# New tables for the split of softmax tiles between ScalarE and VectorE, and for the places of FFN and output tiles

## The chip, the cores and the metric

The kernel runs on one core of a Trainium2 chip. The metric is the device time of one execution in microseconds (us). Before the change three runs took 757.08, 756.82 and 756.5 us, with a median of 756.82 us.

A core has a matrix engine (PE, with its weight loads shown as PEld), VectorE (DVE), ScalarE (ACT), GpSimd (POOL) and SyncE (SP), which here issues DMAs. Each engine works through its own list of instructions in order, and waits on semaphores for the others.

## What is computed

One transformer block in parallel form, with S = 2048 rows, D = 512, 32 heads of 16 that share one K and one V, and a GELU layer of width F = 1792:

```python
xn = layernorm(x)
q = (xn @ wq)            # 32 heads of 16
k, v = xn @ wk, xn @ wv  # one head of 16, shared
p = softmax(q @ k.T * 16 ** -0.5)
attention = (p @ v) @ wo
ffn = gelu(xn @ w1 + b1) @ w2 + b2
out = x + attention + ffn
```

Inputs and output are bf16. The exponentials of the softmax are the largest part: 32 x 2048 x 2048 of them.

## The kernel before

**Tiles and units.** Scores are made transposed, a tile having 128 keys and 512 queries of one head. There are four blocks of 512 queries, eight groups of four heads in each, and 64 tiles to a group (16 blocks of keys by four heads): 2048 tiles. Three tiles make a unit, and there are 683 units. `scores` (L933) puts a unit into three of six PSUM banks with three matmuls (L947) on different rows of PE; units alternate between the two halves of the six banks, so the scores of unit u + 2 cannot start until those of unit u have been read.

**Two ways to an exponential.** A tile is read by ACT or by DVE. ACT applies Exp to all its tiles of a unit in one instruction (L970), one to three tiles wide, and writes bf16 to `E`. DVE takes a different way: L1001 adds a constant to the scores, clamps them and writes int16 to `Dt`, whose bits read as bf16 are a power of two with a straight line in place of the curve. To mend the curve, the weighted sum of five such tiles with different offsets is used. DVE makes the offset copies with integer additions on whole batches (L1047): first one copy of the batch, then, from two copies, two more at once. The last step (L1044) changes one tile at a time in its place, and can go to POOL or to DVE. So a batch of n tiles costs one L1047 of width n, one of width 2n and n instructions of L1044.

**The matmuls with V.** L1014 multiplies a tile by V into one of four column groups of PSUM bank 6. An ACT tile takes one such matmul, a DVE tile five, with V scaled by five different constants.

**The table.** `DTAB` (L60) is a string with one character for each unit, which says which of its tiles go to DVE (`DMASK`, L57): `.` none, `0`, `o` the first, `2`, `t` the last, `a`, `A` the first two, `b`, `B` the last two, `x`, `X` all three. The characters of `CLOSE` (L59: `o`, `t`, `A`, `B`, `X`) end the batch. A batch also ends at six tiles (`KB`) and at the last DVE tile of a group of 64.

**Side work.** Between the units, the kernel does the rest of the block with PSUM bank 7: the projections of q (`q_pack`, L1117), the FFN tiles (`h_mm`, L1146: 16 matmuls and one evacuation by DVE, L1150; 14 of them for each block of 512 queries, 56 in all), and the output tiles (`out_tile`, L1191, and `y_tile`, L1201: the second FFN matmul, the projection of the attention output, the bias and the addition of x; 16 in all). `HP` (L73) and `YP` (L74) hold the unit from which each FFN tile and each output tile may start; an operation placed at u depends on unit u's exponential. x for an output tile is loaded by SP six units ahead. GELU runs on ACT for two blocks at a time, behind units 182 and 512 (`GU`, L75); the FFN tiles of blocks 0 and 1 have to be evacuated by the first, and those of 2 and 3 by the second. No exp of a later unit runs before it.

**The order.** All this is written down as operations with what they read and write. `schedule` (L224) then plays the five engines forward in time with a table of durations and a due time for each operation, and fixes the order of every engine's list; that includes whether an L1044 goes to POOL or to DVE: it may go to POOL beside a DVE instruction that reads PSUM, and DVE takes it where nothing is due earlier. Where PE would be idle for long it adds matmuls with zeros (L1318). The order is fixed when the program is built, and on the chip it cannot adapt.

Of the kernel before, what the change touches and what calls it, by code (L numbers as in the profile page):

```python
# [56 lines left out]
DMASK = {".": (), "0": (0,), "2": (2,), "a": (0, 1), "b": (1, 2), "x": (0, 1, 2),  # L57
         "o": (0,), "t": (2,), "A": (0, 1), "B": (1, 2), "X": (0, 1, 2)}
CLOSE = "otABX"  # L59
DTAB = "20t0220t2..o.02ttt.o.22.to0.2.ot00t2.tt20t.too..222ot2.t.t0.tt2tt0o2.tto.o.ott..oto2ot22.000t0..oot.ot00o.tooot0t.t.200o.0.2o2t..ooo2o20o.ot.o0o..02o..20t2..20tto0o.222o..2220oto02tA2bAoooo02t2o.t22ootoo202oo.22t.tto0t02.o20.o2.to00to..0tto0o22oo22.2tt2o.to0.0toot.tt02.t.2ooo.t202o.t00o0.t2.o22t.0oto00t020o2..o000o0oo.2...02ot00.oo...b...o.2.tt.ooo.0.22at.0t0o.t200.22toob...0t.to..ttto0t..2ootoot02.o0.o..oo2t0to0.ooo2..t02o2.20toot0.o.t220.A.o.0o0.ot.t2.2to0ott20o.2.2222o0.22.0o2ot2...ot.tt..20t02200o00..o.2X2XoBtooo2tt20tt..0o.o0t0t.o.2t2ooto2t.to22tt0t.t.o0o00o.o0.ottt2o200to.2o00.o220.o.2ttt2o2o0.0t02.t0o2.t.2ot.0to0t.2ot02o202o.2.o0ooot2t202o.0oo..o2oo.02tt.22o2.t.2o.o.."  # L60
YF = 664
Y_ALLOW = 8.0
H_ALLOW = 5.0
# [6 lines left out]
EXP_LAT = 0.16  # L70
Q3 = (7, 4, 2)
QK = ((48,88.7,157.4),(45,107.7,130.4),(62,118.7,159.4))
HP = ((15,19,24,26,34,41,45,46,50,52,52,63,81,89),(70.14,86,105.29,106.71,130.86,132.29,141,142.57,157.43,161.86,164.71,167.43,169.14,177.57),(290.86,291,302,305.29,307.71,324.14,341.43,344.57,345.86,358.57,372.71,377.29,378.43,389.14),(428.86,430.14,444,444.43,457.57,458.71,461.14,461.86,466.29,472.57,473.43,479.71,481.29,491))  # L73
YP = ((196,221,243,281),(347,373,383,413),(520,528,530,589),(601,635,641,654))  # L74
GU = ((182, (0, 1)), (512, (2, 3)))  # L75
FG = 7
UB2 = 2
# [449 lines left out]
def bass_parallel_sum__grouped_kv_mqa__dense_activation_gelu__prompt_kernel(  # L527
# [33 lines left out]
    with ExitStack() as es:  # L561
# [584 lines left out]
        def h_mm(tb, ft, ev=EV_ALLOW):  # L1146
            for d in range(DT):
                mm4(pM, w1_sb[:, d, ft * P:(ft + 1) * P], xnT[:, d, tb * TBW:(tb + 1) * TBW], d == 0, d == DT - 1,
                   r=["w1"] + tr(4 * tb, 4 * tb + 4), w=[B(7)], allow=H_ALLOW if tb < NTB - 1 else 1.5)
            dve(lambda e: e.tensor_scalar(ubs[tb % 2][:, ft, :], pM, b1T[:, ft:ft + 1], None, ALU.add),  # L1150
                r=["b1T"], w=M4 + [ukey(tb, ft)], n=TBW + 57, allow=ev)
# [20 lines left out]
        def wo_mm(tb, i, ps, start=False, bk=7, al=1.5):  # L1172
            for n, p in enumerate(ps):
                pp = tb * NGR // 2 + p
                hs = [h for h in range(2) if 2 * pp + h < NTB * NGR - 1]
                assert all(2 * pp + h in onorm for h in hs) and 2 * (pp + NPR) + 1 not in onorm
                mm4(bank(bk), oTp[:, pp % NPR, i * P:(i + 1) * P], wop[:, p, :], start and n == 0, False,
                   r=[("oTp", pp % NPR), "wop"], w=[B(bk)], allow=al)
# [4 lines left out]
        def x_load(tb, i):  # L1183
            ti = tb * 4 + i
            dma("sp", x_sb[:, 14 + i % 2, :], x_view[:, ti, :], f"d_xr{i % 2}", w=[("x", 14 + i % 2)], lat=2.5)
# [5 lines left out]
        def out_tile(tb, i):  # L1191
            y_mm(tb, i, al=Y_ALLOW)
            wo_mm(tb, i, range(NGR // 2), al=Y_ALLOW)
            b2_mm(al=Y_ALLOW)
            xr, key = x_sb[:, 14 + i % 2, :], ("x", 14 + i % 2)
            dve(lambda e: e.tensor_tensor(xr, pM, xr, ALU.add), w=[key] + M4, allow=EV_ALLOW)
            store(tb, i, xr, key)
# [3 lines left out]
        def y_tile(tb, i):  # L1201
            y_mm(tb, i, al=YT_ALLOW[i])
            wo_mm(tb, i, range(FIN_G), al=YT_ALLOW[i])
            b2_mm(stop=i < 3, al=YT_ALLOW[i])
            xr, key = x_sb[:, 14 + i % 2, :], ("x", 14 + i % 2)
            if i < 3:
                dve(lambda e: e.tensor_tensor(xpy[:, i, :], pM, xr, ALU.add), r=[key],
                    w=M4 + [("u", 0, 2 * i), ("u", 0, 2 * i + 1)], allow=EV_ALLOW)
            else:
                mm4(pM, ident, xr, False, False, r=["ident", key], w=[B(7)], allow=YT_ALLOW[i])  # L1210
# [9 lines left out]
        def at(u, fn, cost=0.0):  # L1220
            side.append((u, len(side), fn, cost))

        def q_at(tb, p, u, ps=(), hqs=(), gls=(0, 1)):
            at(u, lambda: q_pack(tb, p, gls), 0.93)
            if ps:
                at(u + 1.5, lambda: q_m(ps, hqs), 0.6)
# [6 lines left out]
        for tb in range(NTB):  # L1233
            u0 = tb * UPT
            if tb > 0:
                for i in range(4):
                    at(YP[tb - 1][i] - 6, lambda tb=tb, i=i: x_load(tb - 1, i))
                    at(YP[tb - 1][i], lambda tb=tb, i=i: out_tile(tb - 1, i), 0.6)
                q_at(tb, 3, u0 + Q3[tb - 1], (2, 3), (4, 5, 6, 7))
            for ft in range(FT):  # L1240
                at(HP[tb][ft], lambda tb=tb, ft=ft: h_mm(tb, ft), 0.66)
            if tb + 1 < NTB:
                for k in range(3):
                    q_at(tb + 1, k, u0 + QK[tb][k], (0, 1) if k == 1 else (), (0, 1, 2, 3))
            else:
                for i in range(4):
                    at(YP[tb][i] - 6, lambda tb=tb, i=i: x_load(tb, i))
                    at(YP[tb][i], lambda tb=tb, i=i: y_tile(tb, i), 0.6)
                at(YF, lambda tb=tb: wo_mm(tb, 3, range(FIN_G, NGR // 2), al=WF_ALLOW))
        side.sort(key=lambda s: (s[0], s[1]))  # L1250

        for u, c in enumerate(DTAB):
            for i in DMASK[c]:
# [5 lines left out]
        for t in range(NTILE):  # L1259
            if is_d[t]:  # L1260
                first, n = (t, 1) if n == 0 else (first, n + 1)
                if n == KB or last_d[t // TPG] == t or (DTAB[t // 3] in CLOSE and not any(is_d[t + 1:t // 3 * 3 + 3])):
                    bsize[first], n = n, 0
# [93 lines left out]
```

## Time and profile before

| what | us |
|---|---|
| three runs | 757.08, 756.82, 756.5 |
| median of the runs | 756.82 |
| span of the profiled execution, first to last instruction | 3410.1 |
| PE busy in it | 3402.4 |
| DVE busy in it | 795.2 |
| ACT busy in it | 808.8 |
| POOL busy in it | 306.0 |

No time of the profiled execution beside its span is given. The page shows a granted TensorE clock of 1.000 for it. Busy time of an engine is the time covered by at least one of its records; a group of instructions is given with its line, engine, operation, tile written and tile read, shapes, count, busy time in us, mean duration in ns, and the idle time of its engine ahead of it with what ended that.

### The profile page before, as it was taken

What the parts mean: (1) busy time and instruction counts of PE and PEld (TensorE: products, weight loads), DVE (VectorE), ACT (ScalarE), POOL (GpSimd) and SP (SyncE); (2) the same over time, 40 slices, a digit from 0 to 9 for tenths busy, and PEclk for the clock granted to TensorE, in tenths of its full rate; (3) what the DMA queues carried; (4) which work ended last, traced back from release to release, by engine and by line L of the source; (5) the groups of instructions that cost most, each with busy time, mean ns of one, the idle gap of its engine ahead of it and who ended that gap; (6) DMA issues with size and microseconds to landing.
All of it is one profiled execution on the core that took longest, in us unless ns stands there. A gap on an engine that the chain in (4) does not pass through costs nothing.

```text
span 3410.1 us, 21709 instructions
## 1 busy us (share of the span) xinstructions
PE 3402.4 (100%) x8948; PEld 426.5 (13%) x8950; DVE 795.2 (23%) x1511; ACT 808.8 (24%) x747; POOL 306.0 (9%) x444
## 2 busy tenths in 40 slices
PE   9999999999999999999999999999999999999999
PEld 4101111111120011001111111101111101111112
DVE  2222222222222222222222222222222222222221
ACT  2222222222222222222222222222221222222221
POOL 1101011110001111110000000000010011110000
DMA  2000000000000000000000000000000000000000
GB/s 82 2 4 7 3 2 4 3 5 4 5 4 3 7 5 8 2 5 5 5 8 5 5 5 1 8 2 7 4 1 12 5 2 7 5 7 5 7 3 7
DMA packets 32075, 23.31 MB, mean 7 GB/s; under 512 B 16369, under 2 KB 27498, under 8 KB 31978
## 3 DMA queue, kind: packets, MB, share of 16 engines
q1 hardware_dynamic: 30922, 21.90, 2.4%
q8 instruction: 71, 1.16, 0.1%
q14 instruction: 26, 0.21, 0.0%
q10 hardware_dynamic: 1056, 0.03, 0.0%
HBM read 13.08 MB, written 2.35 MB: 5 GB/s over the span
## 4 chain that ended last, share of the span: by engine, by line
PE 99%; issue 1%; ACT 0%; DVE 0%; POOL 0%; POOLq 0%
PE pAll L1014 50%; PE pAll L947 27%; PE pAll L661 19%; PE pAll L655 2%; PE pAll L1318 1%; PE pAll L799 1%; PE pAll L1316 0%; PE pAll L1110 0%; ACT xnT L804 0%; DVE x_sb L1150 0%; PE pAll L887 0%; ACT ub L1311 0%; ACT oTp L833 0%; DVE kmr L889 0%; POOL ident L686 0%
## 5 line engine op out<-in xcount | busy, mean ns | idle before, releaser
L1014 PE MATMUL pAll<-Dt,V 128*32 128x512 bf16 x2720 | 1911.2, 1580 | 0.0
L970 ACT ACTIVATE E<-pAll 128x1024 bf16<-128x1024 f32 (+1 forms) x681 | 757.1, 1112 | 2428.9 <-PE pAll L947 2416.5
L1014 PE MATMUL pAll<-E,V 128*32 128x512 bf16 x1504 | 1209.8, 1522 | 0.0
L947 PE MATMUL pAll<-QT,KT 32*128 32x512 bf16 x2048 | 999.4, 1427 | 0.0
L1001 DVE TENSOR_SCALAR Dt<-pAll 128x512 int16<-128x512 f32 (+1 forms) x532 | 374.1, 703 | 2163.6 <-PE pAll L947 2152.3
L1044 POOL TENSOR_SCALAR Dt<-Dt 128x512 int16<-128x512 int16 x389 | 289.5, 744 | 2995.4 <-DVE Dt L1047 1157.5
L661 PE MATMUL pAll<-xnT,w_sb 128*32 128x512 bf16 x896 | 547.7, 1592 | 0.9 <-DVE x_sb L1150 0.9
L661 PE MATMUL pAll<-w_sb,x_sb 128*32 128x512 bf16 x448 | 321.1, 1597 | 0.0
L661 PE MATMUL pAll<-w_sb,ub 128*32 128x512 bf16 x448 | 310.8, 1591 | 0.0
L947 PEld LDWEIGHTS pAll<-QT,KT 32*128 32x128 bf16 x2048 | 98.3, 122 | 1660.5 <-issue 1468.4
L1047 DVE TENSOR_SCALAR Dt<-Dt 128x1024 int16<-128x1024 int16 (+6 forms) x582 | 289.5, 525 | 2.1 <-PE pAll L1014 1.6
L1014 PEld LDWEIGHTS pAll<-Dt,V 128*32 128x32 bf16 x2720 | 203.0, 160 | 666.8 <-issue 625.4
L661 PE MATMUL pAll<-wop,oTp 128*32 128x512 bf16 x256 | 238.8, 1589 | 0.0
L1014 PEld LDWEIGHTS pAll<-E,V 128*32 128x32 bf16 x1504 | 112.4, 143 | 259.8 <-issue 252.4
L661 PE MATMUL pAll<-xnT,wq_sb 128*32 128x512 bf16 x256 | 115.3, 1594 | 0.0
L661 PEld LDWEIGHTS pAll<-xnT,w_sb 128*32 128x32 bf16 x896 | 68.2, 190 | 144.7 <-issue 134.3
L661 PE MATMUL pAll<-b2row,ones 128*32 128x512 bf16 x64 | 83.3, 1618 | 0.0
L1318 PE MATMUL pAll<-xnT,zeros 128*32 128x512 bf16 x84 | 49.2, 1559 | 0.0
L1150 DVE TENSOR_SCALAR ub<-pAll,b1T 128x512 bf16<-128x512 f32 x28 | 21.0, 750 | 107.4 <-PE pAll L661 56.9
L661 PEld LDWEIGHTS pAll<-w_sb,x_sb 128*32 128x32 bf16 x448 | 38.9, 182 | 46.5 <-issue 46.5
L1150 DVE TENSOR_SCALAR x_sb<-pAll,b1T 128x512 bf16<-128x512 f32 x28 | 21.0, 749 | 86.3 <-PE pAll L661 57.0
L1044 DVE TENSOR_SCALAR Dt<-Dt 128x512 int16<-128x512 int16 x155 | 39.4, 283 | 5.9 <-PE pAll L1014 5.9
(120 smaller groups left out, 423.6 us busy)
## 6 DMA issues: line engine op xcount, KB each, us to landing
OfP<-Of SPq DMA_DIRECT2D x124, 32.0 KB, 1.9
rbP<-rden_rows SPq DMA_DIRECT2D x124, 32.0 KB, 1.8
w_sb<-in_B_w_dram SPq DMA_DIRECT2D x2, 1792.0 KB, 12.0
x_sb<-in_A_x_dram SPq DMA_DIRECT2D x8, 256.0 KB, 4.3
x_sb<-in_A_x_dram SPq DMA_DIRECT2D x16, 128.0 KB, 2.1
QT<-qp SPq DMA_DIRECT2D x124, 16.0 KB, 1.8
out_dram<-x_sb SPq DMA_DIRECT2D x12, 128.0 KB, 1.7
wq_sb<-in_A_wq_dram SPq DMA_DIRECT2D x1, 512.0 KB, 6.2
```

Source lines behind the costliest of these rows:

```text
L655: return add("pe", lambda e: e.matmul(o, l, rh, start=start, stop=stop, **kw), r, w, occ=occ, lat=0.23, allow=allow, **ak)
L661: add("pe", lambda e, c=c, j=j: e.matmul(o[c, :], l[:, c], rh, start=start, stop=stop, tile_position=(0, 32 * j)), r, [(k, j) for k in w] ...
L799: add("pe", lambda e, ti=ti, d=d, o=o: e.transpose(pT[:, o:o + P], xn[:, ti % 8, d * P:(d + 1) * P], ident[:]), r=[("u", 0, ti % 8), "iden ...
L947: ins = e.matmul(o, l, rh, start=True, stop=True, tile_position=(q0, 0))
L970: o = act(lambda e: e.activation(E[:, s0:s0 + na, :], bank(b0, na).rearrange("p (a n) -> p a n", a=na), ACT.Exp, scale=LN2 / 128.0), w=[B( ...
L1001: op = dve(lambda e: e.tensor_scalar(Dt[:, s:s + n, :], bank(bk, n).rearrange("p (a n) -> p a n", a=n), float(127 * 128) + SPL_D, SPL_MIN, ...
L1014: add("pe", lambda e, a, b: e.matmul(pO[32 * j:32 * j + 32, :], V1[:, v, kt, :], rhs, start=a, stop=b, tile_position=(0, 32 * j)), r=r + [ ...
L1044: add("pool", lambda e, d=d, k=k: e.tensor_scalar(d, d, 1.0, float(k), ALU.mult, ALU.add), [], [(("D", base[o > 0] + q), o)], occ=PL_OCC, ...
L1047: dve(lambda e, d=view(o, nb), q=view(i, nb), k=k: e.tensor_scalar(d, q, float(k), None, ALU.add), r=keys(i), w=keys(o), n=nb * n * TBW, m ...
L1150: dve(lambda e: e.tensor_scalar(ubs[tb % 2][:, ft, :], pM, b1T[:, ft:ft + 1], None, ALU.add), r=["b1T"], w=M4 + [ukey(tb, ft)], n=TBW + 57 ...
L1318: pr.filler = lambda e, j, o: e.matmul((pO if o else pM)[32 * j:32 * j + 32, :], zeros[:, 0:32], xnT[:, 0, 0:TBW], start=not o, stop=not o ...
```

## The change

Three tables of constants are replaced. `DTAB` has a new string of the same length, 683 characters; `HP` and `YP` have new starting units, 14 for each block of queries in `HP` and four for each block in `YP`. No function is changed. The starting units of the projections of q (`QK`, `Q3`), the units of GELU and all costs and due times of the planner stay.

```diff
-DTAB = "20t0220t2..o.02ttt.o.22.to0.2.ot00t2.tt20t.too..222ot2.t.t0.tt2tt0o2.tto.o.ott..oto2ot22.000t0..oot.ot00o.tooot0t.t.200o.0.2o2t..ooo2o20o.ot.o0o..02o..20t2..20tto0o.222o..2220oto02tA2bAoooo02t2o.t22ootoo202oo.22t.tto0t02.o20.o2.to00to..0tto0o22oo22.2tt2o.to0.0toot.tt02.t.2ooo.t202o.t00o0.t2.o22t.0oto00t020o2..o000o0oo.2...02ot00.oo...b...o.2.tt.ooo.0.22at.0t0o.t200.22toob...0t.to..ttto0t..2ootoot02.o0.o..oo2t0to0.ooo2..t02o2.20toot0.o.t220.A.o.0o0.ot.t2.2to0ott20o.2.2222o0.22.0o2ot2...ot.tt..20t02200o00..o.2X2XoBtooo2tt20tt..0o.o0t0t.o.2t2ooto2t.to22tt0t.t.o0o00o.o0.ottt2o200to.2o00.o220.o.2ttt2o2o0.0t02.t0o2.t.2ot.0to0t.2ot02o202o.2.o0ooot2t202o.0oo..o2oo.02tt.22o2.t.2o.o.."
+DTAB = "t2t22t00202t..22tt..022.to00.t22t00200..o.t..20222o.o2.tot22.2t.t2222tt22..2o222t2..o202o02tt2.o.2.t0.t202.2.20t0toto.2..0ot.t2..ot0o2t02t.2222o.0t...o0ot2020o2.2t0.02.t00.02.20o002..xxXaoto.02oot.0to2tt.0too0.ot0tot.o0o020t0o0.tt20.t22.o0tto..2t2to220oo.22t0.2ooo.o2t2o.0ot0o.t02t022.to0..oot.2t2t.o0002ot.0.2tto.0tt2.02t0.202t.2t.oo.ot0.00t.t0o0.0o0o..o0o22o2.00.t0tot2.0o2.2o.t2o2o.tt22o.0t.0oo.2ot2t2.o0.t0t20to2.2t0t.tt2t.002tt.oo.o0oooo0.2o0o0.t00t2ot2.0t0tt0.oA.o..020tt2t02..t0000...2o..02ot0020o.t2t...00XbXttto200t.tt0o22tt..0t0t222.o2o2.t2t20.t0t0.t0t00t2o.0tt2tot.t000202t2t.o.0to20.0.2o22t0o.2t00o0t0..t02o0.0o.o0ooto.t2t0to.2oo0o222o0022o00.2t.2..t0t2.2t.tttt2.2.to.o.."
-HP = ((15,19,24,26,34,41,45,46,50,52,52,63,81,89),(70.14,86,105.29,106.71,130.86,132.29,141,142.57,157.43,161.86,164.71,167.43,169.14,177.57),(290.86,291,302,305.29,307.71,324.14,341.43,344.57,345.86,358.57,372.71,377.29,378.43,389.14),(428.86,430.14,444,444.43,457.57,458.71,461.14,461.86,466.29,472.57,473.43,479.71,481.29,491))
-YP = ((196,221,243,281),(347,373,383,413),(520,528,530,589),(601,635,641,654))
+HP = ((14.33,26.29,49.54,147.27,14,38.77,51.6,14,34.61,92.18,56.17,130.88,103.7,49),(108.69,82.59,66.39,104.08,133,93.7,109.35,162.93,173.36,139,171.29,159.02,133,137.17),(308.62,328.89,290.1,325,306.98,336.81,316.24,310.73,293.91,381.46,369.7,349,374.48,453.6),(475,473.57,427,468.62,459.3,464.72,451,455.66,491.16,486.09,482.33,480.6,464.72,461.37))
+YP = ((195.26,184.23,228.93,254.61),(353.39,411.43,387.54,421),(516,530.79,566.23,553.42),(600.53,607,655.32,660.47))
```

## The prediction, as it was written before the change was run

> **What bounds the kernel now.** I read the page's head and its chain first, then the groups of ScalarE and VectorE with their shapes kept apart, then the order of time in two short stretches.
>
> ```profile
> span 3410.1 us, 21709 instructions
> ...
> PE 3402.4 (100%) x8948; PEld 426.5 (13%) x8950; DVE 795.2 (23%) x1511; ACT 808.8 (24%) x747; POOL 306.0 (9%) x444
> ...
> PE 99%; issue 1%; ACT 0%; DVE 0%; POOL 0%; POOLq 0%
> ```
>
> The span is 3410.1 us and the three timed runs have a median of 756.82 us. PE's records fill the span, and 3402 us of them cannot lie in a run of 757 us. So PE ran at least some 3402.4 / 756.8 = 4.5 times slower in the profiled execution than in the runs, and the chain, 99% PE, is the chain of that execution alone. No other time of that execution is given; I use its durations on ACT, DVE and POOL as prices, work out differences between the two kernels, and add them to the median of the runs. The waits of this trace are no guide to the runs.
>
> What fills 757 us is seen by adding the records of each engine.
>
> ```profile
> L970 ACT ACTIVATE E<-pAll 128x1024 bf16<-128x1024 f32 x523 | 535.1, 1023 | 1890.8 <-PE pAll L947 1878.5 <-PE pAll L1014 9.3 <-PE pAll L655 2.8
> L970 ACT ACTIVATE E<-pAll 128x1536 bf16<-128x1536 f32 x150 | 217.5, 1450 | 520.3 <-PE pAll L947 520.3
> ...
> L970 ACT ACTIVATE E<-pAll 128x512 bf16<-128x512 f32 x8 | 4.7, 596 | 17.8 <-PE pAll L947 17.8
> ```
>
> ```profile
> 33.76 0.81 ACT L781 ACTIVATE ub<-x_sb,nmr,rstd 128x512 bf16<-128x512 bf16 x1
> 34.47 0.19 ACT L769 ACTIVATE rstd<-lnv 128x2 f32<-128x2 f32 x1
> ```
>
> Back to back, a record on ACT begins before the one ahead of it ends: 33.76 + 0.81 = 34.57, but the next starts at 34.47, 0.10 us earlier. The 681 exps, back to back, then hold ACT for 523 x 0.923 + 150 x 1.350 + 8 x 0.496 = 689 us. All else on ACT (GELU, its table loads, the LayerNorm at the start) is 808.8 - 757.3 = 52 us: some 741 us in all. Of 756.8 us only 16 are left, for the start before x has landed, the end and every wait. **ACT is the first bound.**
>
> The same for DVE, whose rows are these:
>
> ```profile
> L1001 DVE TENSOR_SCALAR Dt<-pAll 128x512 int16<-128x512 f32 x522 | 360.8, 691 | 2108.1 <-PE pAll L947 2104.3 <-PE pAll L655 3.1 <-remote 0.6
> L1047 DVE TENSOR_SCALAR Dt<-Dt 128x1024 int16<-128x1024 int16 x222 | 89.9, 418 | 0.1
> L1047 DVE TENSOR_SCALAR Dt<-Dt 128x2048 int16<-128x2048 int16 x90 | 61.4, 683 | 0.1
> L1047 DVE TENSOR_SCALAR Dt<-Dt 128x3072 int16<-128x3072 int16 x46 | 43.7, 951 | 0.1
> L1047 DVE TENSOR_SCALAR Dt<-Dt 128x512 int16<-128x512 int16 x150 | 41.3, 283 | 0.1
> L1044 DVE TENSOR_SCALAR Dt<-Dt 128x512 int16<-128x512 int16 x155 | 39.4, 283 | 5.9 <-PE pAll L1014 5.9
> L1047 DVE TENSOR_SCALAR Dt<-Dt 128x1536 int16<-128x1536 int16 x41 | 22.5, 550 | 0.1
> L1047 DVE TENSOR_SCALAR Dt<-Dt 128x4096 int16<-128x4096 int16 x18 | 21.8, 1218 | 1.6 <-PE pAll L1014 1.6
> ...
> L1150 DVE TENSOR_SCALAR ub<-pAll,b1T 128x512 bf16<-128x512 f32 x28 | 21.0, 750 | 107.4 <-PE pAll L661 56.9 <-PE pAll L1014 50.4
> ...
> L1001 DVE TENSOR_SCALAR Dt<-pAll 128x1024 int16<-128x1024 f32 x8 | 9.8, 1224 | 43.3 <-PE pAll L947 43.3
> L1047 DVE TENSOR_SCALAR Dt<-Dt 128x6144 int16<-128x6144 int16 x5 | 8.8, 1751 | 0.0
> ...
> L1047 DVE TENSOR_SCALAR Dt<-Dt 128x5120 int16<-128x5120 int16 x5 | 7.4, 1474 | 0.0
> ...
> L1047 DVE TENSOR_SCALAR Dt<-Dt 128x2560 int16<-128x2560 int16 x5 | 4.1, 819 | 0.0
> ...
> L1001 DVE TENSOR_SCALAR Dt<-pAll 128x1536 int16<-128x1536 f32 x2 | 3.5, 1757 | 12.3 <-PE pAll L1014 7.6 <-PE pAll L947 4.7
> ```
>
> ```profile
> L1044 POOL TENSOR_SCALAR Dt<-Dt 128x512 int16<-128x512 int16 x389 | 289.5, 744 | 2995.4 <-DVE Dt L1047 1157.5 <-PE pAll L1014 733.5 <-DVE Dt L1001 646.5
> ```
>
> ```profile
> 1001.54 0.69 DVE L1001 TENSOR_SCALAR Dt<-pAll 128x512 int16<-128x512 f32 x1 [3.12 <-PE pAll L947]
> 1002.15 0.42 DVE L1047 TENSOR_SCALAR Dt<-Dt 128x1024 int16<-128x1024 int16 x1
> ...
> 1022.03 0.68 DVE L1047 TENSOR_SCALAR Dt<-Dt 128x2048 int16<-128x2048 int16 x1
> ...
> 1022.20 0.99 POOL L1044 TENSOR_SCALAR Dt<-Dt 128x512 int16<-128x512 int16 x1 [6.43 <-DVE Dt L1001]
> ...
> 1027.29 0.62 POOL L1044 TENSOR_SCALAR Dt<-Dt 128x512 int16<-128x512 int16 x1 [4.10 <-DVE Dt L1001]
> ```
>
> On DVE the overlap is 1001.54 + 0.69 - 1002.15 = 0.08 us; over the 269 pairs of L1001 and L1047 its median is 0.083. Less this for each instruction, reading scores (L1001) costs 522 x 0.608 + 8 x 1.141 + 2 x 1.674 = 330 us, the additions of L1047 257 us and the 155 of L1044 on DVE 31 us; and all of DVE is at least the page's 795.2 - 1511 x 0.083 = 670 us (the page counts overlapped time once, so this takes off too much). So **DVE is close behind ACT**. But 31 us of it, L1044, can go to POOL, where 389 of 544 already run: DVE has work that it can shed.
>
> **The change part by part.**
>
> *Tiles.* I counted both tables by the rules of the code: characters to tiles, batches closed at six tiles, at a closing letter or at the end of a group. For the table of before this gives exactly the counts of the rows above. For the new one: VectorE tiles 544 to 555; exps of two tiles 523 to 535, of three 150 to 140, of one 8 to 3 (units without an exp: 2 to 5).
> ACT: 12 x 0.923 - 10 x 1.350 - 5 x 0.496 = **-4.9 us**.
> DVE, L1001: singles 522 to 534, pairs 8 to 3, triples 2 to 5: 12 x 0.608 - 5 x 1.141 + 3 x 1.674 = +6.6 us.
> DVE, L1047: 291 batches become 274. By width in units of 512: one 150 to 116, two 222 to 204, three 41 to 38, four 90 to 105, five 5 to 9, six 46 to 44, eight 18 to 17, ten 5 to 9, twelve 5 to 6. At the rows less 0.083: -6.8 - 6.0 - 1.4 + 9.0 + 2.9 - 1.7 - 1.1 + 5.6 + 1.7 = +2.1 us. DVE in all: **+8.6 us** that only DVE can do.
> L1044: 11 more tiles; 0.20 us each on DVE (2.2 us), or 0.62 us each on POOL, whose 306 us leave it room. Which of the 555 go where isn't written in the diff (the planner decides); from none to all 155 on DVE I take a shift to POOL that covers most of the 8.6 us: 8.6 / 0.20 = 43 tiles.
> PE: 11 tiles more by five matmuls in place of one, 44 more in four column groups, 11 waves.
>
> ```profile
> 1005.51 2.55 PE pAll L1014 x2
> ```
>
> Two waves of L1014 in the chain took 2.55 us, 1.28 each; by the factor 4.5 at most 0.28 in a run. 11 waves: between 0 and +3.1 us. I take 0, as PE's share of the runs isn't known and ACT and DVE fill theirs.
> For that the Trainium skill ("TensorE: Matmul & The Clock Gate", section "Wait — 56ns, not 53.3ns?") has 215.7 ns between 512-column matmuls at full clock, by which the 11 waves would be an estimated 2.4 us; the trace, at 1.28 us a wave, doesn't agree and no row here shows such a rate.
>
> *Positions.* All 72 pieces of side work stay, with the same matmuls, evacuations and DMAs; only the unit from which the planner may start them moves. Where they fall decides whether DVE's sum fits under ACT's in each stretch. I put prices from the rows on each unit (exps and GELU for ACT; L1001, L1047 and evacuations at their positions, 0.667 us for an FFN tile and some 0.6 for each other, for DVE), added both over successive stretches, and summed the greater. Over stretches of 5, 10, 20 units this gives 799.0, 763.4, 738.2 before and 792.5, 754.2, 730.0 after: -6.5, -9.2 and -8.2. With a quarter of L1044 on DVE (155 of 544 are 28%) the differences are -5.7, -9.5 and -6.3. These totals are not times, since buffers of two units of scores, and some 19 tiles behind them, smooth more or less than that; but the sign holds for each stretch. Cost of the moves themselves: 0, hidden under ACT as long as each FFN tile is evacuated ahead of the GELU at units 182 and 512. The last start ahead of 182 goes from 177.57 to 173.36, ahead of 512 from 491 to 491.16. If that cover went, each late evacuation would hold ACT 0.67 us (0.750 less the overlap).
>
> *Sum.* ACT gives -4.9 and the stretches at least -5.7; I take -5.3, between them, as ACT is the bound that no buffer relieves: 756.8 - 5.3 = **751.5 us**, the likeliest. Own range 747.5 (the greatest gain of the stretches, -9.5) to 755.
>
> **The rivals.**
> *Nothing won, 756.8 us.* ACT has 4.9 us less to do but waits them out for scores, whose banks DVE's L1001 frees later. For it: 741 of 757 on ACT leave no proof that the 16 us are all start and end. Against: the stretches fall even with L1044 included.
> *DVE takes the bound, slower.* Place: the stretches of dense VectorE tiles. The summed DVE work of units 341 to 511 rises from 169.4 to 173.0 while ACT's falls from 175.8 to 173.6, so nothing is left there for L1044. If POOL takes none more, DVE has 8.6 us more to do: 756.8 + 8.6 = 765.4; if half of the 43, 761. It decides from the point at which POOL takes fewer than some 20 of the 43. For it: on POOL a tile of L1044 took 0.62 us beside an idle DVE and 0.99 us beside a 0.68 us addition, so a fuller DVE makes POOL slower. Against: POOL is busy 306 of 757 us.
> The Trainium skill ("GPSIMD Engine Reference", section "1. Specifications") says that GpSimd shares its SBUF interfaces with VectorE instructions in a 2-port mode; the 0.62 and 0.99 agree.
> *PE is the bound.* The 11 waves then lie on the path: 756.8 + 3.1 = 759.9. For it: PE is 100% busy in the trace. Against: that is at a rate that the runs exclude.
>
> **How the numbers follow.** Differences under 0.2% (1.5 us) can't be told from none. Forecast 0.60; nothing won 0.12; DVE the bound 0.20; PE 0.08. That makes faster 0.60, same 0.12, slower 0.28. The range runs from 747.5 to 761, the price of half a shift: some 0.06 lies below and 0.10 above.
>
> **What would show it.** The group of exps should have 535, 140 and 3 at the same means; L1001 534, 3 and 5. The step on DVE is right if fewer than about 125 of L1044 are on DVE, and wrong if 155 or more stay there with a time of 751 all the same, since DVE then had slack that I deny. If the time falls by much more than 9 us, the waits, not the sums, were the bound; if it rises, DVE or PE was. The profile of after will tell little about waits if PE fills its span again.

## The result, and the profile after

The kernel after takes 750.97 us (median of 4 runs, 750.71 to 751.19) against 756.79 us before; the ratio is 0.9923 with a 95% interval of 0.9909 to 0.9937. That is 5.8 us less, a difference that the interval keeps clear of none, where 5.3 had been predicted. Its profiled execution, unlike that of before, had PE at full speed: the span is 749.0 us in a run of 750.71 us. Head and chain of its page:

```profile
span 749.0 us, 21922 instructions
...
PE 732.8 (98%) x9046; PEld 228.2 (30%) x9046; DVE 736.1 (98%) x1436; ACT 733.2 (98%) x744; POOL 364.4 (49%) x506
...
PE 40%; DVE 30%; ACT 28%; DMA 0%; issue 0%; SPq 0%
```

ACT and DVE are covered by records for all but some 13 to 16 us. For ACT that is what the prediction had put together from the trace of before (all but 16 us); for DVE it had only a lower bound of 670 us. PE's 98% is by itself no sign of a bound; an experiment below adds work to PE. The groups of exps, the reading of scores and the last step L1044 in the same profile, in three views (ACT, DVE, POOL):

```profile
L970 ACT ACTIVATE E<-pAll 128x1024 bf16<-128x1024 f32 x535 | 519.8, 1139 | 0.8 <-PE pAll L947 0.5
L970 ACT ACTIVATE E<-pAll 128x1536 bf16<-128x1536 f32 x140 | 214.5, 1571 | 0.9 <-PE pAll L947 0.7 <-PE pAll L1014 0.2
```

```profile
L1001 DVE TENSOR_SCALAR Dt<-pAll 128x512 int16<-128x512 f32 x534 | 352.2, 675 | 1.0 <-PE pAll L947 0.8
...
L1044 DVE TENSOR_SCALAR Dt<-Dt 128x512 int16<-128x512 int16 x104 | 26.7, 279 | 0.0
```

```profile
L1044 POOL TENSOR_SCALAR Dt<-Dt 128x512 int16<-128x512 int16 x451 | 348.2, 772 | 360.6 <-DVE Dt L1047 143.8 <-PE pAll L1014 93.6 <-DVE Dt L1001 46.2
```

The counts are those of the prediction (535, 140, 534). ACT sat idle ahead of 675 exps for under 2 us. The means of the exps, 1139 and 1571 ns, are longer than the 1023 and 1450 of before, though the instructions are no slower: in a dense stream a record starts while the one ahead still runs. One stretch of the timeline shows it, start, length and count:

```profile
298.56 14.31 ACT L970 ACTIVATE E<-pAll 128x1536 bf16<-128x1536 f32 x14
```

Fourteen exps in 14.31 us: the line names one shape, and three of them are of three tiles, eleven of two. Taken from the end of one record to the end of the next, an exp of two tiles has a pitch of 0.917 us (median; nine tenths of the 535 at most 0.918), one of three tiles 1.343, one of one tile 0.488 (a single case). With these I divide the time of every profile below: from the first instruction to the first exp; the exps, each counted at its pitch; what ends of exps came later than that (waits); the rest between the first and the last exp, which is GELU, its table loads and its waits, and one small other activation; and what follows the last exp. Rows are rounded, so that some miss their span by 0.1.

| profile | to first exp | exps | waits of exps | GELU and rest | after last exp | span |
|---|---|---|---|---|---|---|
| before, PE at full speed | 24.1 | 684.9 | 5.2 | 31.3 | 9.2 | 754.8 |
| after | 24.1 | 680.1 | 3.0 | 32.5 | 9.3 | 749.0 |
| new tiles, old places | 24.6 | 680.1 | 53.8 | 43.5 | 12.6 | 814.6 |
| old tiles, new places | 24.6 | 684.9 | 29.0 | 31.1 | 14.1 | 783.6 |
| after, ten tiles back | 24.7 | 684.3 | 12.6 | 44.4 | 11.9 | 777.9 |
| after, one early tile back | 24.3 | 680.5 | 19.0 | 42.2 | 11.4 | 777.3 |
| that, L1044 moved to POOL | 24.3 | 680.5 | 33.5 | 43.3 | 11.6 | 793.1 |
| after, L1044 moved to POOL | 24.6 | 680.1 | 11.8 | 32.8 | 9.3 | 758.6 |

The first two rows are the account of the change: 4.9 us less of exps (684.95 to 680.08), 2.2 less of waits between them, 1.2 more at the GELUs.

### The profile page after: what moved, and what is told of

Same layout as the page of the kernel before. It is cut to its first block, busy times and chain, and to the rows that moved or that the text cites. A ratio compares the mean times of both kernels' runs of the same rounds, so it can differ in the third digit from the quotient of the medians.

```text
span 749.0 us, 21922 instructions
## 1 busy us (share of the span) xinstructions
PE 732.8 (98%) x9046; PEld 228.2 (30%) x9046; DVE 736.1 (98%) x1436; ACT 733.2 (98%) x744; POOL 364.4 (49%) x506
## 4 chain that ended last, share of the span: by engine, by line
PE 40%; DVE 30%; ACT 28%; DMA 0%; issue 0%; SPq 0%
ACT E L970 28%; PE pAll L1014 19%; DVE Dt L1001 13%; PE pAll L947 13%; DVE Dt L1047 10%; PE pAll L661 7%; DVE x_sb L1150 2%; DVE stats L748 1%; DVE Dt L1044 1%; DVE Of L1059 1%; PE pAll L655 1%; DMA x_sb<-in_A_x_dram 0%; DVE oTp L1086 0%; DVE qp L1122 0%; DVE x_sb L1196 0%
## 5 line engine op out<-in xcount | busy, mean ns | idle before, releaser
L1044 POOL TENSOR_SCALAR Dt<-Dt 128x512 int16<-128x512 int16 x451 | 348.2, 772 | 360.6 <-DVE Dt L1047 143.8
L1014 PE MATMUL pAll<-Dt,V 128*32 128x512 bf16 x2775 | 421.8, 383 | 0.6 <-DVE Dt L1047 0.2
L1001 DVE TENSOR_SCALAR Dt<-pAll 128x512 int16<-128x512 f32 (+1 forms) x542 | 364.1, 688 | 1.0 <-PE pAll L947 0.8
L1047 DVE TENSOR_SCALAR Dt<-Dt 128x1024 int16<-128x1024 int16 (+7 forms) x548 | 288.0, 551 | 0.2
L1014 PE MATMUL pAll<-E,V 128*32 128x512 bf16 x1493 | 284.8, 385 | 0.2
L947 PE MATMUL pAll<-QT,KT 32*128 32x512 bf16 x2048 | 267.2, 384 | 6.2 <-ACT E L970 2.1
L1014 PEld LDWEIGHTS pAll<-Dt,V 128*32 128x32 bf16 x2775 | 110.9, 94 | 119.4 <-issue 72.0
L661 PE MATMUL pAll<-xnT,w_sb 128*32 128x512 bf16 x896 | 122.2, 383 | 0.4 <-DVE x_sb L1150 0.3
L1014 PEld LDWEIGHTS pAll<-E,V 128*32 128x32 bf16 x1493 | 65.9, 94 | 47.5 <-issue 34.7
L661 PE MATMUL pAll<-w_sb,x_sb 128*32 128x512 bf16 x448 | 69.3, 383 | 0.0
L661 PE MATMUL pAll<-w_sb,ub 128*32 128x512 bf16 x448 | 69.3, 383 | 0.0
L661 PE MATMUL pAll<-wop,oTp 128*32 128x512 bf16 x256 | 49.5, 383 | 0.0
L661 PEld LDWEIGHTS pAll<-xnT,w_sb 128*32 128x32 bf16 x896 | 32.1, 95 | 22.4 <-issue 11.8
L1044 DVE TENSOR_SCALAR Dt<-Dt 128x512 int16<-128x512 int16 x104 | 26.7, 279 | 0.0
L661 PE MATMUL pAll<-xnT,wq_sb 128*32 128x512 bf16 x256 | 22.5, 383 | 0.0
L661 PEld LDWEIGHTS pAll<-w_sb,x_sb 128*32 128x32 bf16 x448 | 17.1, 94 | 8.8 <-issue 7.0
L661 PEld LDWEIGHTS pAll<-w_sb,ub 128*32 128x32 bf16 x448 | 17.6, 94 | 4.7 <-issue 2.9
```

The source lines that it names most:

```text
L661: add("pe", lambda e, c=c, j=j: e.matmul(o[c, :], l[:, c], rh, start=start, stop=stop, tile_position=(0, 32 * j)), r, [(k, j) for k in w] ...
L947: ins = e.matmul(o, l, rh, start=True, stop=True, tile_position=(q0, 0))
L1001: op = dve(lambda e: e.tensor_scalar(Dt[:, s:s + n, :], bank(bk, n).rearrange("p (a n) -> p a n", a=n), float(127 * 128) + SPL_D, SPL_MIN, ...
L1014: add("pe", lambda e, a, b: e.matmul(pO[32 * j:32 * j + 32, :], V1[:, v, kt, :], rhs, start=a, stop=b, tile_position=(0, 32 * j)), r=r + [ ...
L1044: add("pool", lambda e, d=d, k=k: e.tensor_scalar(d, d, 1.0, float(k), ALU.mult, ALU.add), [], [(("D", base[o > 0] + q), o)], occ=PL_OCC, ...
L1047: dve(lambda e, d=view(o, nb), q=view(i, nb), k=k: e.tensor_scalar(d, q, float(k), None, ALU.add), r=keys(i), w=keys(o), n=nb * n * TBW, m ...
```

## The experiments

All changes below are against the kernel after unless said otherwise; the kernel before ran beside each group, at 756.7 to 756.8 us.

### The kernel before once more

No edit. 

> The kernel before as it is, for a profile in which PE runs at full speed; the trace of before had PE 4.5 times too slow, and its waits say nothing. Theory (ACT sets the time): ACT has next to no idle time between its first and its last exp, exps of two tiles follow each other at 0.917 us and of three at 1.343 us as in the profile of after, and the stretch of exps is longer than that of after by 12 x 0.917 - 10 x 1.343 - 5 x 0.488 = 4.9 us, taken the other way round, with under 1 us of waits more. Rival (DVE's tiles held ACT up): 2 us or more of ACT's time between exps is waits for scores (L947) that came late because DVE read a bank late. Ratio 1.000 in either case.

It ran in 756.70 us (ratio 1.000, 0.999 to 1.0009), and its profile has a span of 754.8 us where the one shown with the prediction had 3410.1. Head of its page, then its L1044 on DVE and on POOL from the groups of all engines:

```profile
span 754.8 us, 21711 instructions
...
PE 736.8 (98%) x8950; PEld 233.1 (31%) x8950; DVE 738.1 (98%) x1511; ACT 738.0 (98%) x747; POOL 314.5 (42%) x444
```

```profile
L1044 POOL TENSOR_SCALAR Dt<-Dt 128x512 int16<-128x512 int16 x389 | 298.1, 766 | 416.9 <-DVE Dt L1047 160.1 <-PE pAll L1014 76.2 <-DVE Dt L1001 48.6
...
L1044 DVE TENSOR_SCALAR Dt<-Dt 128x512 int16<-128x512 int16 x155 | 39.1, 279 | 0.0
```

ACT is busy for 738.0 us; the prediction had worked out some 741 from the trace with the slower PE. Exps are 0.917 and 1.343 apart here too. The waits are 2.2 us more than after, over the 1 us that the theory had allowed and at the 2 us that its rival had named. So ACT's sum is most of the gain and not all of it. Whether DVE's late reading of a bank made these waits, as the rival has it, is not shown: around two of the longest, the chain has PE at work on L1014 and L661 right up to the score matmuls. From before to after, L1044 on DVE falls from 155 to 104: 51 tiles, 10.2 us, went to POOL, against the 8.6 us that the new tiles put on DVE. DVE's busy time falls by 2.0 us (738.1 to 736.1).

### Tiles and places apart

```diff
 DTAB: new
-HP, YP: new
+HP, YP: as before
```

> The new table of tiles with the old starting units of FFN and output tiles. Theory: the ACT sum is that of after, 4.9 us under before; the places only decide whether DVE keeps up. If the places matter little: 751 to 752 us (ratio 0.993). If tiles and places were fitted to each other, DVE falls behind in the stretches where evacuations now meet dense tiles, and part or all of the 4.9 us is lost to waits of ACT: 754 to 760. Rival that the places alone made the gain: 756 or more and no stall of ACT beyond that of before.

814.29 us, ratio 1.0761 (1.074 to 1.0781): 63 us more than after, far outside what was expected. Exps wait 53.8 us, and 28 of it is one wait. ACT's timeline around it, the chain of waits in that stretch (start, us, what), and two stretches with the busy time of PE, PEld, DVE, ACT and POOL, the clock, and DMA:

```profile
574.05 9.39 ACT L970 ACTIVATE E<-pAll 128x1536 bf16<-128x1536 f32 x8
611.65 1.02 ACT L970 ACTIVATE E<-pAll 128x1024 bf16<-128x1024 f32 x1 [28.21 <-PE pAll L947]
612.69 1.28 ACT L1162 ACT_TABLE_LOAD   x1
```

```profile
588.82 1.15 PE pAll L661 x16
...
590.00 0.76 DVE x_sb L1150
...
590.80 1.15 PE pAll L661 x16
...
607.61 2.00 PE pAll L661 x16
...
609.63 0.76 DVE x_sb L1150
```

```profile
590.00:600.00 10.00, 5.65 (x64) 1.50 (x64) 3.61 (x6) 0.00 (x0) 0.00 (x0) 0.75 0.14 30
600.00:610.00 10.00, 6.73 (x50) 1.49 (x50) 3.56 (x7) 0.00 (x0) 0.00 (x0) 0.50 0.06 15
```

The FFN tiles of the last blocks have piled up ahead of the second GELU; nine of them, and one projection of q, stand between the two exps. They pass one at a time through PSUM bank 7: 16 matmuls (1.15 us), then the evacuation on DVE (0.76), then the next tile's matmuls, with the last score matmuls behind them in PE's list. ACT has nothing to do for 28 us. PE is busy for only 5.65 of the first 10 us shown. Its granted clock falls to a mean of 0.75 in that stretch and to 0.50 in the next, and there the 16 matmuls take 2.00 us, which draws the pile out further. (The Trainium skill, "TensorE: Matmul & The Clock Gate", section "What's actually happening", says that PE's clock is set by how busy PE has been recently and is halved when it idles; the 0.50 agrees, with a PE that idled only in part.)

```diff
-DTAB: new
+DTAB: as before
 HP, YP: new
```

> The old table of tiles with the new starting units. Theory: ACT has its old sum, so no gain is to be had: 756.8 at best, and 757 to 762 if tiles and places were fitted to each other. Rival (the places made the gain): 752 to 754.

785.29 us, ratio 1.0378 (1.0362 to 1.0393). No pile in front of a GELU this time (GELU and rest 31.1), but 29.0 us of waits, 22.7 of them in 16 pieces of 0.5 to 4 us, and L1044 on DVE 194 times. So neither half of the change is worth anything alone: the new tiles need the new places.

### Ten tiles back to ACT, one early, one late

```diff
-DTAB[u] = "0" or "2"   # u = 53, 104, 161, 249, 309, 370, 437, 496, 578, 632
+DTAB[u] = "."
```

> The kernel after with ten single VectorE tiles, spread over the units, given back to ACT: ten exps go from two tiles to three. Theory (ACT sets the time): 10 x (1.343 - 0.917) = 4.3 us more, 755.2. Rival (DVE sets it, or both do alike): DVE has some 10 us less to do and the time stays or falls, 749 to 752.

780.57 us, ratio 1.0318 (1.0302 to 1.0333). The exps grow by the expected 4.3 us (680.1 to 684.3), and some 25 us come on top: waits of exps, of the GELUs and behind the last exp. So the theory's sum held and its conclusion did not. Two further runs changed one tile only.

```diff
-DTAB[53] = "2"   # in the other run DTAB[632] = "2"
+DTAB[53] = "."   # in the other run DTAB[632] = "."
```

> The kernel after with one VectorE tile, in unit 53 of 683, given back to ACT; the planner orders everything behind it anew. By the sum of ACT alone: +0.43 us, 751.4. Theory after the first four runs (tables and places are fitted to one exact order, and a change spoils the order of everything behind it): some 10 to 30 us more, 761 to 781, with waits of ACT and of GELU throughout.

> The kernel after with one VectorE tile, in unit 632 of 683, given back to ACT. By the sum of ACT alone +0.43 us. Theory (the tables are fitted to one exact order, and a change spoils what is planned behind it): only 50 units lie behind this one and no GELU, so +0.4 to +3 us, 751.4 to 754, against the +28 us of the tile in unit 53. Rival (any single change of the table costs some 25 us, wherever it is): 765 or more.

The early tile costs 28.3 us (779.28 us; 1.0296, 1.0281 to 1.0312), the late one 0.1 us (751.07 us; 0.9925, 0.991 to 0.994), for the same 0.43 us of exps. The two fit the theory that what matters is how much of the order is planned anew behind the place. They do not tell it apart from another: behind the late tile lies no GELU either. In the profile of the early tile L1044 is on DVE 167 times (104 in after), 12.6 us more of it at 0.2 us each, and FFN tiles come late to the GELU. Both profiles around the last part of the first GELU, after first:

```profile
222.24 3.19 ACT L1162 ACTIVATE x_sb<-x_sb 128x3584 bf16<-128x3584 bf16 x1 [0.51 <-DVE x_sb L1150]
```

```profile
228.56 3.19 ACT L1162 ACTIVATE x_sb<-x_sb 128x3584 bf16<-128x3584 bf16 x1 [5.15 <-DVE x_sb L1150]
```

The last FFN tile is evacuated 0.51 us late in after and 5.15 us late here. In the four kernels with a new order from early on DVE holds more of L1044 (209 with the old places, 194, 175 with ten tiles back, 167), and the times go the same way (814, 785, 781, 779); with the late tile it is 108, at 751. That two numbers go together doesn't say which makes which; the last experiments try it.

### A microsecond more on each engine, at the same order

These edits are made where the instructions are issued and the planner doesn't see them, so every engine's list stays that of after. First ACT:

```diff
-activation(E, scores, Exp, scale=LN2 / 128)
+activation(E, scores, Exp, scale=LN2 / 128, bias=epsc[:, 0:1])   # units u % 7 == 3
```

> The kernel after, with the order of all engines as it is (the planner is not told). 97 of the 678 exps, those of every seventh unit, get a bias read from a column of 1e-5, which makes the instruction longer by some amount d that the profile will show (estimate 0.09 us, the step between the ACT records of 0.19 and 0.28 us in the start of the profile of before, the one without and the other with a bias column). Theory (ACT sets the time): the time grows by 97 x d, some 8.7 us, to 759.7, as ACT has no idle time to take it. Rival (DVE or PE sets it): less than half of it.

The groups of exps without and with the bias:

```profile
L970 ACT ACTIVATE E<-pAll 128x1024 bf16<-128x1024 f32 x457 | 463.1, 1189 | 0.6 <-PE pAll L947 0.5
...
L970 ACT ACTIVATE E<-pAll,epsc 128x1024 bf16<-128x1024 f32 x78 | 98.6, 1264 | 0.0
```

By the ends of the records the pitch rises from 0.917 to 0.998, so d is 0.081 us, and 97 x 0.081 = 7.9 us of ACT were added. The time is 756.69 us, 5.7 more than after: 0.73 us for each added microsecond. The column of waits, which counts the addition, rises from 3.0 to 8.7 us: some 2 us of the waits that were there took up the rest.

Then DVE, with a memset ahead of L1001:

```diff
+memset(dm[:, 0:32], 0.0)      # units u % 5 == 3; in the later run dm[:, 0:128]
 tensor_scalar(Dt, scores, ...)
```

> The kernel after, same order. DVE does a memset of 32 columns ahead of the score reading (L1001) in 95 units, every fifth, some 0.1 us each by the 0.065 us that the DVE rows have beside their columns: some 9.5 us more work on DVE. Theory: DVE is 98% busy in the profile of after, but 104 of L1044 in it fill gaps; at a fixed order those gaps are gone, so DVE binds nearly as much as ACT: 4 to 9 us more (755 to 760). If ACT alone is the bound: under 2 us more.

751.67 us, 0.7 more. By itself that would have said that DVE has slack; but the edit was much smaller than meant. Memset and L1001 together have a pitch of 0.610 us against 0.599 for L1001 alone, 0.011 more, 1.05 us in all, though the memset's record is 85 ns long. So it was made again with 128 columns.

> As the run with a memset of 32 columns on DVE at a fixed order, but 128 columns: the 32 columns had added 0.011 us to the pitch of DVE each (0.610 against 0.599), 1.05 us in all, as most of them lay in the shadow of the next instruction; 96 columns more at 0.96 columns a ns add 0.10 us each, so 95 x 0.11 = 10.5 us of DVE work. Theory (DVE binds beside ACT at a fixed order): by the 0.70 us that 1.05 us had cost, +7 us, 758. If DVE has slack: under 2 us more.

```profile
L1003 DVE MEMSET dm<- 128x128 f32 x95 | 15.7, 165 | 0.0
```

757.05 us, 6.1 more than after. The pitch of the two is 0.685, 0.086 more, so 8.2 us of DVE work were added: 0.74 us for each microsecond, the same as on ACT. Waits of exps rise from 3.0 to 8.5 us. This is the price of more work on DVE. What less work would win is another matter: ACT waits only 3.0 us between exps and 1.3 us at the GELUs in after, so not much more than that is to be had.

Then PE:

```diff
+matmul(o[:, 0:224], l, rh[:, 0:224])   # ahead of the first score matmul, units u % 7 == 3
 matmul(o, l, rh) for the three tiles
```

> The kernel after, same order. In 98 units, every seventh, the first score matmul is preceded by one of 224 columns into the same bank, some 0.093 us each at the rate of 0.213 us for 512 columns that the profile of after shows: 9.1 us more work on PE, in front of scores that ACT waits for next. Theory (PE isn't the bound, and the prediction's 0 for its 11 waves stands): under 1.5 us more. Rival (PE is on the path: the chain of after has it for 40%): 4 to 9 us more.

751.30 us, 0.33 more for some 9 us of matmuls (estimated from the pitch of 0.22 us for 512 columns): PE has slack at these places. So the 40% of the chain that the page gives to PE is not 40% of the time that would grow with PE's work.

### L1044 from DVE to POOL

The order is kept, and L1044 that the planner had put on DVE goes to POOL at the same place in the list.

```diff
 pr.schedule()
+for op in every second or third (fourth) of the L1044 on DVE:
+    op.eng = op.stream = "pool"
```

> The kernel with the one tile in unit 53 given back, its order kept, but 63 of its 167 L1044 on DVE, every second or third, are put on POOL in the same place of the order: 104 stay on DVE as in after, and DVE has 63 x 0.2 = 12.6 us less to do. Theory (what the tile cost was DVE's work: the planner left 63 more L1044 on DVE): 8 to 20 us of the 28 go, 759 to 771. Rival (the order of FFN tiles and scores itself is spoilt, and DVE's waits are a sign of it only): within 4 us of 779.

> The kernel after, order kept, with 26 of the 104 L1044 on DVE, every fourth, put on POOL: 5.2 us less on DVE. Theory (ACT sets the time): ACT's waits between exps are only 3.0 us and those of GELU 1.2 us in the profile of after, so 0 to 4 us less, 747 to 751. Rival (POOL, at 0.77 us an instruction and busy for half of the span, hands these tiles to PE later than DVE did): 751 to 755.

Both went against the theory, and beyond the bounds of its rivals too. The kernel with the early tile rose from 779.28 to 793.47 us (1.0489, 1.0473 to 1.0505), after with 26 tiles moved from 750.97 to 760.15 us (1.0044, 1.0027 to 1.0061). DVE's groups in the profile of after, then in that with the 26 moved:

```profile
L1047 DVE TENSOR_SCALAR Dt<-Dt 128x1024 int16<-128x1024 int16 x204 | 82.2, 414 | 0.1
...
L1047 DVE TENSOR_SCALAR Dt<-Dt 128x3072 int16<-128x3072 int16 x44 | 41.4, 943 | 0.0
L1047 DVE TENSOR_SCALAR Dt<-Dt 128x512 int16<-128x512 int16 x116 | 31.0, 278 | 0.0
L1044 DVE TENSOR_SCALAR Dt<-Dt 128x512 int16<-128x512 int16 x104 | 26.7, 279 | 0.0
```

```profile
L1047 DVE TENSOR_SCALAR Dt<-Dt 128x1024 int16<-128x1024 int16 x204 | 84.5, 426 | 0.2
...
L1047 DVE TENSOR_SCALAR Dt<-Dt 128x3072 int16<-128x3072 int16 x44 | 42.1, 959 | 0.0
L1047 DVE TENSOR_SCALAR Dt<-Dt 128x512 int16<-128x512 int16 x116 | 32.5, 290 | 0.1
L1044 DVE TENSOR_SCALAR Dt<-Dt 128x512 int16<-128x512 int16 x78 | 23.3, 317 | 0.0
```

DVE lost 26 x 0.2 = 5.2 us of work and gained in these four rows 204 x 0.012 + 44 x 0.016 + 116 x 0.012 + 78 x 0.038 = 7.5 us: and its busy time rises from 736.1 to 741.0 us. Which of its instructions lost the time is seen when the pitch of each L1047 and L1044 on DVE is set against the lower quartile of its own shape, by what POOL was doing.

Where POOL's record starts while the DVE instruction runs, DVE loses next to nothing (250 cases in after, 0.1 us in sum). Where POOL is already in the record of an L1044 that has over 0.2 us still to go, one of two things happens. Either DVE stands still for what is left of POOL's record, less 0.05 us: 2 cases and 0.3 us in all before, 4 cases and 0.8 us in after, 24 cases and 8.7 us with 26 tiles moved (0.16 to 0.52 us each), 48 cases and 19.0 us with 63 moved in the kernel with the early tile. Or POOL stands still and DVE loses nothing: 29 cases with 26 tiles moved. An L1044 on POOL takes 0.62 us undisturbed. In after, 213 of the 451 have a record of over 0.7 us, and 201 of these end 0.47 to 0.49 us after the end of an L1047 or L1044 on DVE. So, but for some 0.1 us, the two do not work at the same time; one stands still until the other is done. (The Trainium skill, "GPSIMD Engine Reference", section "1. Specifications", says that the two engines share their SBUF interfaces and contend in certain DVE modes; the trace agrees, and adds that one waits for the other and how long.)

DVE's account alone does not make up the 9.2 us that the 26 tiles cost. It is 5.2 us less of L1044 against 7.9 us more of standing still, 2.7 us more, some 2 us of time at the 0.74 from above. The rival put on record for this run, that POOL hands tiles to PE later, is seen at the largest new wait of ACT:

```profile
228.43 2.66 POOL L1044 TENSOR_SCALAR Dt<-Dt 128x512 int16<-128x512 int16 x1 [0.63 <-DVE Dt L1044]
...
228.87 1.74 DVE L1047 TENSOR_SCALAR Dt<-Dt 128x6144 int16<-128x6144 int16 x1
...
232.56 1.02 ACT L970 ACTIVATE E<-pAll 128x1024 bf16<-128x1024 f32 x1 [2.37 <-PE pAll L947]
```

An L1044 on POOL stands behind an L1047 of 1.74 us on DVE and ends after 2.66 us. The matmul with V that needs its tile (L1014, at 231.15) starts after it, then the rest of a group of side matmuls and the score matmuls behind it in PE's list, and ACT waits 2.37 us. This is one place, with 2.5 of the 8.8 us that the waits grew by; how the rest divides between DVE's standing still and late tiles is open.

So the run with the early tile could not show whether its 12.6 us of DVE work or the late FFN tiles were the cause of its 28 us: the cure added a fault of its own. That stays open.

## Why the prediction was right, and where it was not

**The main term was right.** ACT's sum was forecast at -4.9 us. The exps at their pitch went from 684.95 to 680.08, -4.9, and the experiment on ACT shows that ACT's work sets the time, at 0.73 for each added microsecond. The step from that trace to the runs, that ACT's records add up to nearly all of 757 us and PE's cannot, was confirmed by the profile of before at full speed (ACT 738.0 us). For DVE the sum was well short: at least 670 us, where the profile has 738.1. The signs named for this term came out in the counts (535, 140, 3; L1001 534, 3, 5) and not in the means, which rose, as shown above, without a slower instruction.

**DVE as the second bound was right, and so was its way out.** The tiles put 8.6 us more on DVE. The prediction let the planner move most of 43 L1044 to POOL; it moved 51, and DVE's busy time fell by 2.0 us. With 104 on DVE, under the 125 that had been named, the slower rival did not come to pass. That more work on DVE costs like more on ACT is shown by the 0.74 of the longer memset. But the reason given, that POOL has room at 306 of 757 us, was not enough: an L1044 on POOL and an instruction from SBUF to SBUF on DVE stand in each other's way. The planner puts an L1044 on POOL beside a DVE instruction that reads PSUM, and with the new tables it found such places for 51 more: DVE stood still 4 times in after, 2 times before. The 26 moved without regard to it cost 9.2 us, by DVE's standing still and by tiles that POOL hands over late.

**PE at 0 was right**: some 9 us of matmuls, put ahead of scores and not where the new tiles have theirs, cost 0.33 us. The rival at 759.9 is excluded by the result.

**The step on the positions failed.** It had put the cost of the moves at 0, "hidden under ACT as long as each FFN tile is evacuated ahead of the GELU", and had drawn a gain of at least 5.7 us from sums over stretches of units, whose "sign holds for each stretch". Such sums over ten units, worked out again from the prices that the prediction names, come out within some 1 us of that of after for the new tiles with the old places and for the one early tile; these ran 63 and 28 us slower. Such sums see how much work falls into a stretch and not in which order it must pass, and here the order decides: the pile of FFN tiles in front of a GELU, and scores that reach ACT 0.5 to 4 us late many times over. The number survived because only 0.4 us of the 5.3 came from that step, and because the new places were fitted to the new tiles, of which the sums say nothing; that is luck. Beyond ACT's sum the runs show -2.2 us of waits and +1.2 us at the GELUs, -1.0 in all; that this is near to the -0.4 is luck too, and what made the waits shorter is open. (The low end of the range is a slip of 0.2 us: 756.8 - 9.5 is 747.3.)

**The rival "nothing won" was wrong**, but not for the reason given against it, the stretches: most of the 16 us that the prediction could not place are not waits for scores. Of the 24.1 us up to the first exp ACT is busy for 19.0, and of the 9.2 us behind the last exp for 1.0, so that 13.3 us without work lie at the two ends. Waits of exps were 5.2 us before, and the 4.9 us could not go into them: they fell to 3.0.

## What to carry to other kernels

When two engines run nearly without gaps, a change can be priced by what it takes off the sum of each of them, from the counts and the pitch of their instructions, even with a profile whose third engine ran at the wrong speed. The sum is a floor of the time: whether the kernel comes near it hangs on the order, and here a table that was fitted to one order lost almost 4% when one early entry was changed, so such tables are changed and tested together. To find which engine binds, lengthen a few of its instructions without changing the order, and measure in the profile how long the addition really was. Work that is moved between engines without asking the planner can meet a conflict that the planner's rule had kept away.

## What the runs showed that was not expected

- The same kernel was profiled once with waves of 512-column matmuls 1.28 us apart and once with 0.22, and its span was 3410.1 and 754.8 us; the page gave a mean clock of 1.000 for the one and 0.998 for the other. ACT and DVE had nearly the same speed in both (an exp of two tiles 0.923 and 0.917 us, an L1001 0.608 and 0.599).
- A memset of 32 columns in a dense stream of DVE cost 0.011 us, one of 128 columns 0.086 us, though their records are 85 and 165 ns long.
- A bias column makes an exp 0.081 us longer.
- An L1044 on POOL and an L1047 or L1044 on DVE, both from SBUF to SBUF, hardly work at the same time. One waits for the other: DVE up to 0.52 us with 26 tiles moved, and POOL, whose record includes its wait, up to 2.66 us in all where 0.62 is enough undisturbed.
